# S4 convolution beside a 16-head expert layer on one core: parameters in three parts of channels, gelu for two head groups at once, and tiles from own lists of slots

## The chip, the cores and the metric

The kernel runs on one core of a Trainium2 chip. A core has a matmul engine (TensorE, PE in the profile, with its weight loads listed as PEld), an elementwise engine (VectorE, DVE), an engine for activations (ScalarE, ACT), GpSimd (POOL), which here issues the gathers, and SyncE (SP), which issues most DMA transfers. Each engine works through its own instructions in program order and waits at an instruction until what it needs is there. SBUF is the memory on the chip with 128 partitions; PSUM holds the matmul results in eight banks of 128 x 512 float32.

The metric is device time in microseconds for one execution. Before the change three runs took 755.45, 764.48 and 769.52 us, median 764.48.

## The reference

```python
x  = A_u                                   # 2048 tokens x 448 channels
xn = _layernorm(x)
return x + _A_ref(xn, ...) + _B_ref(xn, ...)

def _A_ref(u, ...):                        # S4 convolution, 256 states per channel
    dt = exp(log_dt); logdA = dt * (A_re + 1j * A_im); dB = dt * (B_re + 1j * B_im)
    K = einsum("dn,dnl,dn->dl", Cc, exp(logdA * l), dB).real     # kernel of length 2048
    y = irfft(rfft(u) * rfft(K))[:2048] + u * Dskip              # causal convolution
def _B_ref(x, ...):                        # 16 heads, one expert of 64 x 64 each
    q = einsum("nd,dhc->nhc", x, w_q)
    s1 = q1 @ k1.T ; s2 = q2 @ k2.T        # 64 scores each, per head
    e = argmax(s1) * 64 + argmax(s2)       # the best of both halves (top 1)
    act = gelu(sum_d(x * u[e]))            # tanh form
    out = sum_h(act * v[e])                # softmax over one candidate is 1
```

## The kernel before, in words

Tokens are cut into 16 tiles of 128. The two halves of the work share all engines and run interleaved.

**The expert half.** The query weights are folded into the keys at the start: for each of 16 heads SP loads w_q in two tiles of 448 KB (L855), PE multiplies them with the keys (wc, L862), ScalarE takes the result out of PSUM (L866), PE transposes it (L875), and ScalarE writes the table W (L881 to L883). Per token tile, PE transposes the normalized tokens (L943) and forms 2048 scores (sc, L961 and L970), VectorE takes maxima (mx, L985) and finds the indices (L992 to L1006). GpSimd then gathers for each token and head one row of u and v side by side, 3584 bytes (ue, L1083). With 32 tokens by 4 heads on the partitions, one token tile needs 16 gathers: 4 groups g of heads by 4 columns c. VectorE forms a dot product per gather (L1091), ScalarE the square and the tanh of gelu (L1098, L1104), VectorE the small steps between (L1101, L1110, L1107, tiles of 128x4) and the product with a mask (A, L1114); PE adds up the v rows (po, L1121), and ScalarE takes them out (ob, L1133). So 64 chains of gelu are formed, one for each tile and group, each behind four gathers.

**The convolution half.** At the start the S4 parameters are worked out for all 448 channels at once, states on the partitions, in tiles of 128x896 (L432 to L499, on VectorE, ScalarE and GpSimd): weights, phases as integers and logarithms of magnitudes. exp(log_dt) is computed from 112x4 values (L364 and on), stored to DRAM and loaded back over all partitions. The phases go to DRAM as tp_d (L502) and the split exponents as tt_d (L508); every four of 56 batches of 8 channels load their share back (tpl, L540; ttl, L520). A batch forms phase rows (ph, L610, L614), sines and cosines on ScalarE (CS, L629 to L635), magnitudes by matmul and Exp (lg L579, mg L590), their products (zi and mg, L660 to L666), and on PE the kernel blocks kp (L682) and VK (L702, L706). The convolution of a chunk of channels then runs on PE with products on VectorE (U L798, us L803, cp L808, ip L830), its output goes through DRAM (t_d, L842; tl, L1149), is multiplied once more (po, L1159) and added to the output by a GpSimd DMA (L1167).

**The order.** The program is a set of streams of steps. A string ORDER, one character per step, fixes the order in which steps are issued, and with it the order on each engine. A step names rings it takes from and gives back to; the rings only count. The tiles themselves come from pools: 25 tiles of 4096 bytes (pool "q") serve the token tiles, W, the gathers, and the tiles of the convolution; PSUM tags kv and s2 have three banks each, tp, po, vk and others one.

```python
t = s.q.tile([128, 1024], F32, name=name, tag="q", bufs=s.NQ)
y = p.add("e_g", "GATHER", xf(128, 3584), ga, deps=[s.ix_done[t]], take=("ue",))
y = p.add("e_p", "PE", 830, m2, deps=[y], take=("po",) if g == 0 else (), give=("A", "ue", "ue", "ue", "ue"))
```

Of the kernel before, what the change touches and what calls it, by code (L numbers as in the profile page):

```python
# [22 lines left out]
NB = 8  # L23
# [92 lines left out]
class Plan:  # L116


    def __init__(s):
        s.streams, s.left, s.phys = {}, {}, {}  # L120

# [26 lines left out]
    def run(s):  # L148
# [3 lines left out]
        for ch in ORDER:  # L152
# [25 lines left out]
    "zUIygU!#ISh!h#yyyISRzKRVROizWx$W$%yyfziHHhNgxSfSzxPxKLISiz!#JM#RjRLRSfI!$$%QzIhhgTJfiIziGISSzMfykI!#yIyU#RUi&hRhh!yI$S$i"
    "dIeRXUSzUO%jhSIUNSlizIIhPkhLRhQzISMLhTMyRdiLzibURe!yyRzMfUzlyUiU##NY!U$$%LShSgJRjyRZZSifMhKhgHzz!UzKxiHfSfaN#Ufyy(LJ!Skh"
    "M#$hOPgUzxUiSL$%RRSyhhyymzxHTMhmlizxUUSRhhhn!nhHjhkhgLMURiUSLhhUyz#gRyRQV1iziSIiNI!fiIzz!ifSYclmISfhM#fQ$I$%hnSSgO#IyTWf"  # L180
    "IiUzjhiKZPhHI!&hRmUIhR#QkW$UhnI$UyyyyUzIzlzU%!hHjRy#z!iziS#Iy$RS$hkJyyyL%ZiUSzzHHdMhyRyLMelIbROzISz!I#!Iy#$SygiPfIhiSSXm"
    "zfzhRJmRUfRU$%L!nITnjhgfi#SIUIfMLhIhMkUIUiSgRRR#h!ISli$$N%OIJjKxcNJhzxyyVhhcyyxSzzSyUySUxzSzh!TPi#h!h#QmULUWZ$aih&Kyyhnf"
    "$UfURfU%MRziSzUgyzyLhNMhRgifSLfRQz!hSiH(yhg#HWzz#h!$R$hhbjZzz%Riyh!k#y!#MHYO$SSd$%iyHPIhekSizIIUSzlliIiRRLjhIKQghTzIUiSh"
    "UIR!#UihISMkhKyIyyfI!UI#URlmyS$I$fURfSShnJVY%NcgROhKxhfSajXxUizzyyPiSxzgLkhyymRQixzz!M#z#N!$Rhym$lhzfinyL&%RTSyzy(njUSUz"
    "hUz!yhhgzhzMU#Uhk!!SWR##il$$fh!Ri%R#hzhJfyi$yzfyxz$OzyfgxSxxS%KfimSiSiUhhP!gL#RMRhjhL#TiUiyUWSd!z$hRUSyzRMR$yy%yhkhSiyhS"
    "izUnjzhkilSROUNY(Qzlh!zhSzUPy&#!y#ymiSR$z$egyUb%hny!h#!aRyzTizfzUgzSfyyRURSXfiUR#$NQSU$UROzUihSSxoz!xYhgmzSf%yzSyP#h#Uy!"
    "h!hyfURRjnhTiRkhhS$U#hyS$y%UiymjUzilk!#UlxV$$xg%&hzzz!zzWh#!(Sn#hRSyyzyiz!iyyRmRS#V#$Wh!my$$inno$fUoyfigSSph%hzfgp%zfzUq"
    "rzqzyyphYj!hhzUrizfiyTkqpqroz#rhhhi#!!dpjqlW#$hrebiUh#kst$!hpg%pqWhxh$iorfoo$qltUxpgypyfzrhqxhciXfUg%irszijhUyifq&pzfrUi"
    "yhkhyyxy(zlzU!thozy#p#!qzz$hy$pjq!hr##iy!z$cay%yhhiyg$yUzfyUhzfqhrzhkpz%qr!pyyygUVzrtWihhuqppl#zfzyghrfi#!hy!ms(#fd#$yqm"
    "hyu!hr$%nqteth$ii$irnyiymjYbxxmhxsihnkxKnhjii%tzhWilgfhhYt&ykzgzzQffzzzz!yhhgh#if#yy!l$fmmh!$#h#!izz%iji$ynhyyuhnhyzkhhl"  # L190
    "z$zzihjgfhzi!hf#z!kayfli#gfifib$ih!hg$mhhuhijd%#hi)heh)(ym!nini#*ki$ljhxzXm%i+hhkf$xzxlxngh%hmgyyyizzifi&f!ynhhjgyy#yyhh"
    "i!khflf#zh$h*$y+hjmnkhca%hzziiilmnYyzg!hiz#y!hhzzyf#$zjgh$chzfykg%yh!zfzfifihdhzl#!hmi#i!eh##nh)o*+jb$i$!i$hg$ihk,%%ix)x"
    "lhhyh*zfmjx+niiyYygykhhyzff,aiyyyzyilgyxy,,yXyzzf!h&zhjmyfklgnz#o#h!zmyhy!n$$p#p!#hhhhqzhq$%zih$izpzizifr%jqprzhpgqrifzf"
# [11 lines left out]
class Kernel:  # L205
# [1025 lines left out]
```

## Time and profile before

| what | value |
|---|---|
| median of three runs | 764.48 us |
| the profiled execution | 763.02 us |
| its span, first to last instruction | 761.1 us |
| mean granted TensorE clock | 0.915 of full |
| busy: PE, DVE, ACT, POOL | 652.1, 669.5, 552.9, 360.7 us |
| ACT table loads at L639 and L590 | 28 and 26, 1283 ns each |
| DMA moved | 211.83 MB, mean 278 GB/s |

The profile lists groups of instructions with busy time, mean duration and the idle time of the engine just before them, with what ended it. Windows give busy time by engine for a stretch of the span, with the granted clock, the mean busy share of the 16 DMA engines, and GB/s. The chain that ended last follows the last instruction back through what released each step.

### The profile page before, as it was taken

The page shows a single profiled execution, that of the slowest core. Times are in us where ns is not written, and L with a number is a line of the kernel's source. Part 1 is how long each engine was busy: PE and PEld are TensorE (multiplying, and loading weights), DVE is VectorE, ACT ScalarE, POOL GpSimd, SP SyncE. Part 2 cuts the span into 40 slices and gives each one's busy share as a digit, 9 for nine tenths or more (in the row PEclk, how much of TensorE's full clock was granted, in tenths as well). Part 3 has the DMA queues.
Part 4 walks back from the last instruction along what each step waited for, and adds up shares of the span by engine and source line. Part 5 has one row for each costly group of instructions (what it writes and reads, how often), then busy time and mean ns, then how long its engine had stood idle before and what let it go on. Part 6 is the DMA issues. An engine that isn't in the chain of part 4 may idle for free.

```text
span 761.1 us, 19861 instructions
## 1 busy us (share of the span) xinstructions
PE 652.1 (86%) x7628; PEld 355.8 (47%) x7628; DVE 669.5 (88%) x1691; ACT 552.9 (73%) x1137; POOL 360.7 (47%) x307
## 2 busy tenths in 40 slices
PE   1999999999999999999887958679996587899882
PEld 0344333443444444444465734346763344576751
DVE  4896578999999999999999999999998999999840
ACT  3886147566876886774796898888898888999630
POOL 2011024544363645655447686484564657752523
PEclk9999999999999999999999877688987756999995
DMA  9998656978687896887989999899898999977998
GB/s 324 328 374 305 228 136 254 355 238 246 221 257 266 252 327 191 309 255 257 337 300 340 281 324 361 263 327 279 265 342 271 308 325 286 339 248 209 296 178 128
DMA packets 119095, 211.83 MB, mean 278 GB/s; under 512 B 38937, under 2 KB 94233, under 8 KB 118937
## 3 DMA queue, kind: packets, MB, share of 16 engines
q0 software_dynamic: 31232, 124.80, 51.6%
q1 hardware_dynamic: 87768, 85.77, 35.2%
q8 instruction: 60, 0.98, 0.5%
q14 instruction: 35, 0.28, 0.1%
HBM read 180.90 MB, written 33.29 MB: 281 GB/s over the span
## 4 chain that ended last, share of the span: by engine, by line
PE 41%; DVE 29%; ACT 14%; DMA 7%; issue 6%; SPq 1%; POOL 1%; POOLq 0%; DVEq 0%; ACTq 0%
PE sc L961 14%; DVE ue L1091 6%; PE U L798 3%; PE po L1121 3%; DVE mg L666 3%; DVE zi L662 3%; DVE ph L614 3%; PE kp L682 3%; PE sc L970 3%; DMA ue<-in_uv_dram,ig 3%; PE ip L830 2%; PE wc L862 2%; PE up L724 2%; ACT CS L629 2%; DMA VU<-vu_d 2%
## 5 line engine op out<-in xcount | busy, mean ns | idle before, releaser
L1083 POOL DMA_INDIRECT ue<-in_uv_dram,ig x256 | 312.6, 1221 | 309.0 <-PE po L1121 72.9
L961 PE MATMUL sc<-W,xt 128*128 128x512 f32 x384 | 180.1, 608 | 2.2 <-ACT xt L946 1.9
L1091 DVE SCALAR_TENSOR_TENSOR ue<-ue,xr 128x448 f32<-128x448 f32 x256 | 154.1, 617 | 4.0 <-DMA ue<-in_uv_dram,ig 4.0
L961 PEld LDWEIGHTS sc<-W,xt 128*128 128x128 f32 x384 | 69.7, 191 | 91.9 <-issue 83.9
L1121 PE MATMUL po<-ue,A 128*32 128x448 f32 x512 | 68.6, 616 | 9.4 <-DVE A L1114 5.0
L590 ACT ACTIVATE mg<-lg 128x512 f32<-128x512 f32 x112 | 63.4, 600 | 11.1 <-PE lg L579 10.6
L682 PE MATMUL kp<-mg 128*32 128x64 f32 x1792 | 62.3, 237 | 7.9 <-DVE kt L693 3.1
L666 DVE TENSOR_TENSOR mg<-mg,CS 128x1024 f32<-128x1024 f32 x56 | 68.2, 1217 | 0.0
L662 DVE TENSOR_TENSOR zi<-mg,CS 128x1024 f32<-128x1024 f32 x56 | 68.2, 1217 | 0.0
L635 ACT ACTIVATE CS<-CS,halfpi 128x1024 f32<-128x1024 f32 x56 | 64.5, 1152 | 0.8
L614 DVE CUSTOM_DVE_ANT_0 ph<-st,ph 128x512 uint16<-128x512 uint16 (+2 forms) x84 | 64.9, 772 | 0.2
L629 ACT ACTIVATE CS<-ph 128x1024 f32<-128x1024 int32 x56 | 62.6, 1118 | 1.4 <-issue 0.5
L632 ACT ACTIVATE CS<-ph 128x1024 f32<-128x1024 int32 x56 | 63.2, 1128 | 0.0
L682 PE MATMUL kp<-zi 128*32 128x64 f32 x1792 | 61.6, 234 | 0.0
L682 PEld LDWEIGHTS kp<-mg 128*32 128x32 f32 x1792 | 45.2, 119 | 29.2 <-issue 11.7
L579 PE MATMUL lg<-lc,rt 32*128 32x512 f32 x112 | 39.8, 548 | 21.5 <-ACT mg L590 17.5
L702 PE MATMUL vp<-f,kt 128*64 128x128 f32 x448 | 43.6, 326 | 16.5 <-ACT tl L1163 5.0
L985 DVE TENSOR_REDUCE mx<-sc 128x8 f32<-128x512 f32 x64 | 43.6, 682 | 14.6 <-PE sc L970 9.2
L682 PEld LDWEIGHTS kp<-zi 128*32 128x32 f32 x1792 | 47.2, 121 | 0.1
L798 PE MATMUL U<-VU,g 128*64 128x128 f32 x384 | 42.3, 301 | 5.4 <-DVE cp L808 2.7
L702 PEld LDWEIGHTS vp<-f,kt 128*64 128x64 f32 x448 | 28.9, 160 | 38.3 <-issue 11.9
L862 PE MATMUL wc<-wq,kk 128*64 128x448 f32 x128 | 31.7, 586 | 17.1 <-DMA wq<-in_wq_dram 17.1
(244 smaller groups left out, 1242.2 us busy)
## 6 DMA issues: line engine op xcount, KB each, us to landing
wq<-in_wq_dram SPq DMA_DIRECT2D x32, 448.0 KB
xr<-xn_d SPq DMA_DIRECT2D x64, 224.0 KB
vu_d<-vst SPq DMA_DIRECT2D x64, 112.0 KB
VU<-vu_d SPq DMA_DIRECT2D x12, 512.0 KB
t_d<-tq SPq DMA_DIRECT2D x24, 256.0 KB
tl<-t_d SPq DMA_DIRECT2D x12, 512.0 KB
ue<-in_uv_dram,ig POOLq DMA_INDIRECT x256, 6.4
xx<-in_x_dram SPq DMA_DIRECT2D x16, 224.0 KB
```

The costliest lines, as they stand in the source:

```text
L614: s.nc.vector.tensor_tensor(out=rw(n, 2 * n), in0=rw(0, n), in1=o["st"][:, k, b0:b0 + 2].rearrange("p b h m x -> p (b h m x)")[:, None].to ...
L629: s.nc.scalar.activation(CS[:, 1].rearrange("p (m r x) -> p m r x", r=16, x=2), four(s.ph), AF.Sin, scale=SC)
L635: s.nc.scalar.activation(B["CS"][:, 0], B["CS"][:, 0], AF.Sin, scale=-SC, bias=s.halfpi)
L662: V.tensor_tensor(out=zi[:, 512:], in0=mg[:, 512:], in1=CS[:, 1], op=ALU.mult)
L666: V.tensor_tensor(out=mg[:, 512:], in0=mg[:, 512:], in1=CS[:, 0], op=ALU.mult)
L682: s.nc.tensor.matmul(kp[32 * c:32 * c + 32, 64 * gi:64 * gi + 64], T[ri][:, 1024 + m:1056 + m], view(T[ri], m, [[512, 2], [1, 32]]), start ...
L702: s.nc.tensor.matmul(vp[64 * ri:64 * ri + 64, 128 * gi:128 * gi + 128], B["kt"][:, 64 * gi:64 * gi + 64], s.f1[:, ri], start=True, stop=True)
L798: s.nc.tensor.matmul(U[64 * h:64 * h + 64, sl, ri], s.g[q][:, 2 * kk + h, ri], src[:, k1 + h, :w], start=True, stop=True)
L961: s.nc.tensor.matmul(B["sc", q].rearrange("p a b -> p (a b)"), B["xt"][:, i], w, start=(q % 2 == 0 and i == 0), stop=(q % 2 == 1 and i == 2))
L1083: s.nc.gpsimd.indirect_dma_start(out=ue, out_offset=None, in_=s.io["uv"], in_offset=bass.IndirectOffsetOnAxis(ap=s.IDX[t][:, c, g:g + 1].b ...
L1091: s.nc.vector.scalar_tensor_tensor(Q["ue", c][:, :D], Q["ue", c][:, :D], 1.0, B["xr", c], op0=ALU.mult, op1=ALU.mult, accum_out=Q["dot"][: ...
L1121: s.nc.tensor.matmul(B["po"][32 * c:32 * c + 32, :D], Q["A"][:, c], Q["ue", c][:, D:], start=(g == 0), stop=(g == 3))
```

## The change

1. **Parameters in parts.** Channels are cut into parts of 128, 160 and 160. Each part has its six inputs packed into one array, loaded as two transfers, and goes through the same arithmetic on tiles of 256, 320 and 320 columns. Part 0 stays on chip: its phases (`R1`) and split exponents (`tt`) are read by the batches where they were formed. Parts 1 and 2 go through tp_d and tt_d as before. exp(log_dt) is computed on 128x448 after one broadcast load, with no way through DRAM.
2. **Gelu for two groups.** From token tile 4 on (`PT=4`) one chain serves two head groups: eight gathers and dots, then small steps on 128x8 and a mask product of 128x256, then two groups of po matmuls. Tiles 0 to 3 keep one chain per group.
3. **Own lists of slots.** The 25 tiles of 4096 bytes and the banks of kv, s2 and tp are allocated once. `run` takes the index that was freed first when a step takes from a ring, and `rel` in a step's code says which tile it frees.
4. A new ORDER string, and 2048 instead of 4096 for the DMA scratch size.

```diff
+PARTS = (128, 160, 160)
...
                 s.left[s.phys[tag]] -= 1
+                if s.phys[tag] in s.free:
+                    s.got.setdefault(tag, []).append(s.free[s.phys[tag]].pop(0))
...
-    "4HH4HH44441444Z4444H606HH414144114H72III2II72II2I2I7728I8I2IJJ22I2I2I2I72KIZ414I82852I24K4I4COP224C4234LMLDHMHHH4LMDCLM4"
+    "013ZHH3HH314Z3353153H33116633HH3H322I2222I2I2II2I2III222I2222I7IJJI3K7IICI7788I2IIL8DC332699I798M7874I77OC8DEC77778I7I9D"
...
+    def slot(s, *tags):
+
+        for tag in tags:
+            if s.p.got.get(tag):
+                r, i = s.p.phys[tag], s.p.got[tag].pop(0)
+                return s.own[r][i]
+    def rel(s, *views):
+
+        for v in views:
+            s.p.freed.append(s.where[v.tensor.name])
...
-            T["ld"] = s.sm.tile([112, 4], F32, name="ld")
-            s.nc.sync.dma_start(T["ld"], io["log_dt"].rearrange("(p f) -> p f", f=4))
+            s.nc.sync.dma_start(T["ld"], io["log_dt"].rearrange("(o f) -> o f", o=1).to_broadcast([128, D]))
...
-        N = 2 * D
-        B = s.pb = {} if part == 0 else s.pb
-        hold = ("cs", "cs", "zi", "zi", "mg", "mg", "c3", "c3", "c3", "vk")
+        d0, w = s.parts[k]
+        N, nb, b0 = 2 * w, w // NB, d0 // NB
+        keep = k == 0
...
+        P["tp_done"] = [c1] if keep else [stp(0, 0, "A_re", [f2]), stp(0, 1, "T3", [ph]), stp(1, 0, "B_im", [f1]), stp(1, 1, "T1", [c1])]
...
-                s.nc.tensor.transpose(o["ps"][:, t], o["tl"][:, t], s.ident)
+                s.nc.tensor.transpose(o["ps"][:, t], P["tt"][t][:, i:i + 4].rearrange("p b k -> p (b k)") if P["keep"] else o["tl"][:, t], s.ident)
...
+            if P["keep"]:
+                o["tp"] = P["R1"][:, :, :, i:i + 4]
...
-        for g in range(4):
+        w = 2 if t >= s.o["PT"] else 1
+        for g0 in range(0, 4, w):
...
+                            for k in ("dot", "x2", "th", "dw"):
+                                Q[k] = s.sm.tile([128, 2, 4], F32, name=k, bufs=2)[:, :w]
...
+            yA = p.chain("e_v2", "DVE", [(75, v2), (dv(128 * w), v2c)], deps=[y, yw, s.C["mask"]], take=("A",), give=("gel",))
+            for g in range(g0, g0 + w):
+                def m2(g=g, g0=g0, Q=Q):
...
+                    s.rel(*[Q["ue", g, c] for c in range(4)])
+                y = p.add("e_p", "PE", 830, m2, deps=[yA], take=("po",) if g == 0 else (), give=(("A",) if g == g0 + w - 1 else ()) + ("ue",) * 4)
```

**What moves, in three places.** The first is SP's list at its start, before. Here pw and pv are parameter tiles, xx token tiles, ld log_dt, kk the keys.

```order
L892 DMA xx<-in_x_dram 128x448 x2
L419 DMA pw<-in_C_im_dram 128x896
L419 DMA pw<-in_B_im_dram 128x896
L419 DMA pv<-in_C_re_dram 128x896
L419 DMA pv<-in_B_re_dram 128x896
L294 DMA ld<-in_log_dt_dram 112x4
L419 DMA pv<-in_A_im_dram 128x896
L419 DMA pv<-in_A_re_dram 128x896
L892 DMA xx<-in_x_dram 128x448 x3
L309 DMA kk<-in_k_dram 128x2x64 x2
L272 DMA ident<-in_ident_dram 128x128
L855 DMA wq<-in_wq_dram 128x896
```

After, a name q with a number is one of the 25 slots; the rows from the lc table to the first two wq loads are shown (ahead of them stand the broadcast of log_dt and four token tiles).

```order
L355 DMA lcf<-in_lc_dram 128x768
L969 DMA q_85<-in_x_dram 128x448
L969 DMA q_86<-in_x_dram 128x448
L342 DMA kk<-in_k_dram 128x2x64
L441 DMA q_87<-in_par_dram 128x1024
L342 DMA kk<-in_k_dram 128x2x64
L359 DMA wtf<-in_wt_dram 128x64
L448 DMA q_88<-in_par_dram 128x2x256
L311 DMA ident<-in_ident_dram 128x128
L929 DMA q_90<-in_wq_dram 128x896
L929 DMA q_91<-in_wq_dram 128x896
```

The six full parameter loads give way to the two of part 0, now behind the token tiles and just ahead of the weights.

The second place is ScalarE in the same stage. Before, the Square, Abs and Sqrt of all channels (L446 to L450) stand in front of the first evictions of PSUM (xt L946, vst L727, wt L866):

```order
L446 ACTIVATE pv<-pw 128x896
L447 ACTIVATE pw<-pw 128x896
L925 ACTIVATE xx<-xx,q,y 128x448 x2
L448 ACTIVATE pv<-pw 128x896
L450 ACT_TABLE_LOAD
L450 ACTIVATE pw<-pv 128x896
L329 ACTIVATE lc<-lcf 128x768
L946 ACTIVATE xt<-xtp 128x512
L727 ACTIVATE vst<-up 128x448
```

After, they are those of part 0 (L486 to L490), and the exponents' first copies (L498) and the arctangent (L516) stand between evictions (L941 for wt, L788 for vst, L1023 for xt):

```order
L486 ACTIVATE q_87<-q_88 128x256
L487 ACTIVATE q_87<-q_88 128x256
L488 ACTIVATE q_87<-q_88 128x256
L941 ACTIVATE wt__250<-kv_104 128x448
L490 ACT_TABLE_LOAD
L490 ACTIVATE q_87<-q_87 128x256
L788 ACTIVATE q_97<-tp_110 128x448
L498 ACTIVATE q_89<-q_88 128x16x8
L364 ACTIVATE wt<-wtf 128x64
L498 ACTIVATE q_89<-q_88 128x16x8
L941 ACTIVATE wt__285<-kv_105 128x448
L516 ACT_TABLE_LOAD
```

Each table load and each wait of part 0 on ScalarE now has evictions behind it that PE's next matmuls need.

The third place is VectorE. Its list around the first product zi of the first batch, before (mx maxima, A the mask product, q and y of the layernorm):

```order
L1091 SCALAR_TENSOR_TENSOR ue,dot<-ue,xr 128x448
L985 TENSOR_REDUCE mx<-sc 128x8
L1107 SCALAR_TENSOR_TENSOR th<-th,dw 128x4
L920 SCALAR_TENSOR_TENSOR y<-q,y 128x2
L1114 TENSOR_TENSOR A<-mask,th 128x128
L918 TENSOR_TENSOR q<-y 128x2
L992 TENSOR_TENSOR eq<-sc,mx 128x512
L660 SCALAR_TENSOR_TENSOR zi<-mg,CS 128x512
```

and after (s with a number is a score bank):

```order
L669 TENSOR_SCALAR ph<-q_88 128x2x2x16 x2
L501 TENSOR_TENSOR q_99<-q_98,q_99 128x20x8
L1065 TENSOR_REDUCE mx<-s_108 128x8
L1111 SCALAR_TENSOR_TENSOR ix<-cm,tf 128x8x4
L1072 TENSOR_TENSOR q_83<-s_108,mx 128x512
L673 ISA ph<-ph,st 128x256
L1120 TENSOR_TENSOR top<-top 128x32
L719 SCALAR_TENSOR_TENSOR zi<-mg,CS 128x512
```

The phase rows read part 0's tile (q_88) instead of a reloaded one, steps of another part (L501) stand among them, and 17 score maxima stand ahead of this zi, where 15 did.

In the second half, the gelu steps of VectorE before:

```order
L1110 TENSOR_TENSOR dw<-dot,ig 128x4
L1091 SCALAR_TENSOR_TENSOR ue,dot<-ue,xr 128x448
L614 ISA ph<-ph,st 128x256
L1091 SCALAR_TENSOR_TENSOR ue,dot<-ue,xr 128x448
L660 SCALAR_TENSOR_TENSOR zi<-mg,CS 128x512
L1107 SCALAR_TENSOR_TENSOR th<-th,dw 128x4
L614 ISA ph<-st,ph 128x512
L1114 TENSOR_TENSOR A<-mask,th 128x128
L693 TENSOR_TENSOR kt<-kp,dsk 128x2
L1101 SCALAR_TENSOR_TENSOR x_7339<-x_7339,dot 128x4
L1110 TENSOR_TENSOR dw<-dot,ig 128x4
```

and after:

```order
L1186 SCALAR_TENSOR_TENSOR x_5960<-x_5960,dot 128x8
L1176 SCALAR_TENSOR_TENSOR q_97,dot<-q_97,xr 128x448
L1195 TENSOR_TENSOR dw<-dot,ig 128x8
L673 ISA ph<-st,ph 128x1024
L1176 SCALAR_TENSOR_TENSOR q_98,dot<-q_98,xr 128x448
L1192 SCALAR_TENSOR_TENSOR th<-th,dw 128x8
L1176 SCALAR_TENSOR_TENSOR q_85,dot<-q_85,xr 128x448
L1199 TENSOR_TENSOR A<-mask,th 128x256
```

Two chains of four small rows each have become one, and more dots stand between its steps.

More of the change, by code (lines that the diff above doesn't have):

```diff
@@ L165, in run @@
             st.fn()
+            if sorted(r for r, _ in s.freed) != sorted(s.phys[tag] for tag in st.give if s.phys[tag] in s.free):
+                raise RuntimeError("slots: " + k)
+            for r, i in s.freed:
+                s.free[r].append(i)
+            s.freed = []
         if any(pos[k] < len(s.streams[k]) for k in names):
@@ L178 @@
[L178 to L181, printed above, removed]
@@ L235, in alloc @@
         s.vkp = pool("vkp")
-        s.q = pool("q", s.NQ)
+        s.q = pool("q")
         s.ps = pool("ps", 1, space=bass.MemoryType.PSUM)
+        s.own = dict(ue=[s.q.tile([128, 1024], F32, name="q%d" % i) for i in range(s.NQ)])
+        for tag, n in s.bufs.items():
+            s.own[tag] = [s.ps.tile([128, 512], F32, name="%s%d" % (tag, i)) for i in range(n)]
+        s.where = {}
+        for r, l in s.own.items():
+            s.p.free[r] = list(range(len(l)))
+            for i, t in enumerate(l):
+                s.where[t[:, :8].tensor.name] = (r, i)
         dr = pool("dr", 1, space=bass.MemoryType.DRAM)
@@ L425, in params @@
+        held = 3 if keep else 4
+        l1 = p.add("par_ld", "SP", xf(128, 4 * N * per), ld1, take=("ue",))
+        l2 = p.add("par_ld", "SP", xf(128, 4 * N * (6 - per)), ld2, take=("ue",) * (held - 1))
         d1, d2 = dv(N), dv(N, 2)
@@ L516, in exponents @@
         o = {}
+        i = 4 * g - P["b0"]
         def l():
@@ L607, in f @@
                 b0 = b % 4
+                if k == 3 and b % 4 == 2 and "ue" in o["give"]:
+                    s.rel(o["tp"])
                 if k < 0:
```

357 lines of the change are left out of this document (204 added, 153 removed).

## The prediction

> **What bounds the kernel now.** I began with the page's first two parts: totals, then the span in forty slices.
>
> ```profile
> span 761.1 us, 19861 instructions
> PE 652.1 (86%) x7628; PEld 355.8 (47%) x7628; DVE 669.5 (88%) x1691; ACT 552.9 (73%) x1137; POOL 360.7 (47%) x307
> PE   1999999999999999999887958679996587899882
> DVE  4896578999999999999999999999998999999840
> PEclk9999999999999999999999877688987756999995
> ```
>
> No engine is full on average, but the slices are not alike: TensorE (PE) is full up to about slice 19, VectorE (DVE) from slice 7 to slice 37. Averages over stages hide this, so next come 20-us windows; the five pairs are PE, PEld, DVE, ACT, POOL with busy time and instruction count, then clock, DMA share, GB/s.
>
> ```profile
> 60.00:80.00 20.00, 20.00 (x81) 8.69 (x82) 10.70 (x16) 8.56 (x26) 2.23 (x1) 1.00 0.90 328
> 80.00:100.00 20.00, 18.79 (x55) 7.70 (x54) 10.39 (x16) 5.68 (x21) 0.00 (x0) 1.00 0.41 136
> 100.00:120.00 20.00, 19.31 (x56) 7.67 (x55) 16.32 (x39) 8.32 (x24) 9.17 (x9) 1.00 0.77 251
> 120.00:140.00 20.00, 20.00 (x67) 7.39 (x66) 17.56 (x62) 15.82 (x36) 10.53 (x9) 1.00 0.67 224
> 300.00:320.00 20.00, 20.00 (x146) 8.18 (x143) 19.97 (x53) 14.57 (x30) 12.88 (x12) 1.00 0.88 272
> 440.00:460.00 20.00, 11.63 (x183) 7.29 (x186) 18.60 (x53) 18.09 (x35) 15.68 (x14) 0.69 0.99 346
> 500.00:520.00 20.00, 14.58 (x254) 9.26 (x246) 17.21 (x49) 16.44 (x30) 16.66 (x14) 0.83 1.10 307
> 560.00:580.00 20.00, 12.31 (x178) 7.32 (x182) 15.78 (x45) 18.84 (x34) 6.93 (x7) 0.68 0.89 325
> ```
>
> Three stages follow. Up to 140 us PE is full and DVE is not: these four windows leave DVE 80 − 54.97 = 25.0 us idle. From 140 to about 360 both are full. From 360 to 720 PE falls to 12 to 15 us in 20 in the quoted windows while DVE stays near 20; there DVE sets the pace, and in the dips neither does. The last slice (19 us) holds no DVE work: a chain of transfers. The chain that ended last agrees (by engine, by line, some of its pieces):
>
> ```profile
> PE 41%; DVE 29%; ACT 14%; DMA 7%; issue 6%; SPq 1%; POOL 1%; POOLq 0%; DVEq 0%; ACTq 0%
> by line: PE sc L961 13.6%; DVE ue L1091 6.3%; issue 5.9%; PE U L798 3.2%; PE po L1121 3.1%; DVE mg L666 3.0%; DVE zi L662 2.9%; DVE ph L614 2.8%; PE kp L682 2.7%; PE sc L970 2.6%; DMA ue<-in_uv_dram,ig 2.6%; PE ip L830 2.5%; PE wc L862 2.4%
> 3.56 6.87 DMA ld<-in_log_dt_dram
> 447.58 8.55 DMA ue<-in_uv_dram,ig
> 512.87 6.16 DMA ue<-in_uv_dram,ig
> 550.22 4.82 DMA ue<-in_uv_dram,ig
> 736.01 4.91 DMA t_d<-tq
> 741.06 2.89 DMA tl<-t_d
> ```
>
> PE's largest item is the score matmuls, DVE's are dots and products, and 2.6% (20 us) is gathers whose landing was awaited, 19.5 us of it in the three pieces shown, two of them in windows where DVE dips.
>
> **The change, part by part.** All sums stand against this execution: 763.02 us, its span of 761.1 and 1.9 us around it. It lies 1.5 us below the median of 764.48; the shown runs spread by 14 us, so 2% (15 us) is about what a measurement can tell from no change.
>
> *Gelu for two groups.* The first view is groups by line (busy, mean ns, idle before), the second a stretch of DVE's timeline, start and duration.
>
> ```profile
> L1101 DVE SCALAR_TENSOR_TENSOR x<-x,dot 128x4 f32<-128x4 f32 x64 | 9.9, 154 | 6.3 <-ACT x L1098 6.0
> L1110 DVE TENSOR_TENSOR dw<-dot,ig 128x4 f32<-128x4 f32 x64 | 10.0, 157 | 0.0
> L1107 DVE SCALAR_TENSOR_TENSOR th<-th,dw 128x4 f32<-128x4 f32 x64 | 9.9, 154 | 5.0 <-ACT th L1104 4.1
> L1114 DVE TENSOR_TENSOR A<-mask,th 128x128 f32<-128x128 f32 x64 | 18.3, 287 | 2.7 <-PE po L1121 2.0
> L1091 DVE SCALAR_TENSOR_TENSOR ue<-ue,xr 128x448 f32<-128x448 f32 x256 | 154.1, 617 | 4.0 <-DMA ue<-in_uv_dram,ig 4.0
> L1104 ACT ACTIVATE th<-x 128x4 f32<-128x4 f32 x64 | 13.3, 208 | 13.8 <-DVE x L1101 13.7
> ```
> ```profile
> 132.24 0.15 DVE L1101 SCALAR_TENSOR_TENSOR x<-x,dot 128x4 f32<-128x4 f32 x1
> 132.31 0.16 DVE L1110 TENSOR_TENSOR dw<-dot,ig 128x4 f32<-128x4 f32 x1
> 132.38 0.28 DVE L1003 TENSOR_TENSOR eq<-eq 128x256 bf16<-128x256 bf16 x1
> ```
>
> From token tile 4 on, 48 chains become 24. Three small DVE instructions go per merged pair. A listed duration is 0.155 us, but the next instruction starts 0.07 us later, so one is worth 0.07 on a full engine: 24 × 3 × 0.07 = 5.0 us (11.2 by listed durations). The mask product A: from 128 to 448 columns the rows go from 287 to 617 ns, about 1.03 ns a column, so 128x256 is near 0.42 us, against 2 × 0.287: 0.155 listed per pair, or 0.07 by starts; 24 × 0.07 = 1.7 us (3.7 listed). Together 6.7 us, up to 14.9. I take 6.7, since DVE is full there. "Perfetto Trace Analysis" of the Trainium skill, section "Optimizing Scalar/DVE Operations", says a DVE instruction on SBUF carries about 60 ns of overhead and that profiled latency is about twice this since half overlaps the next instruction. The trace agrees (0.07 from start to start, 0.155 listed); by its 60 ns the saving would be an estimated 24 × 4 × 0.06 = 5.8 us, by the full latency the larger sum.
>
> Each chain also waits twice for ScalarE, 11.3 us over 64; 24 fewer give 4.2 if the wait per chain stays. Together 10.9 us. Between 220 and 360 us, where roughly a quarter of these chains lies (judged from the tiles' spread), PE is full and hides the gain; so 8 us reach the end, with 0 as the other end if the order refills the gaps. On ScalarE 48 activations go: 48 × 0.208 = 10 us, in cover.
>
> *Gather slots.* A pair holds eight slots of 4096 bytes, where a single held four, until its po matmuls; part 0 holds two of 25 until its last steps are formed. The waits and the DMA issues:
>
> ```profile
> POOL ue L1083 <- PE po L1121: 72.9, 23, 9.5
> ue<-in_uv_dram,ig POOLq DMA_INDIRECT x256, 6.4
> ```
>
> GpSimd waits for a slot today, 9.5 us at worst, and DVE hardly notices: 4.0 us before 256 dots. So slots are tight with cover. Doubling the 20 us of awaited landings is the upper end; the lower is that the 4.0 us vanish, because the own list hands out the slot that was freed longest ago. I take +2, near the small row. PSUM lists I cost at nothing: number and length of the PE instructions stay, and a bank's release is still its last reader; they share the gather term's ends.
>
> *Parameters in parts.* About 31 DVE instructions of 128x896 become three each, of 256, 320 and 320 columns; the 19 for log_dt go from 112x4 to 128x448; 10 table loads come on ScalarE.
>
> ```profile
> L438 DVE SCALAR_TENSOR_TENSOR pv<-pw,pv 128x896 f32<-128x896 f32 x2 | 2.2, 1092 | 0.1
> L435 DVE TENSOR_SCALAR pv<-pv 128x896 f32<-128x896 f32 x2 | 1.2, 623 | 0.0
> L639 ACT ACT_TABLE_LOAD x28 | 35.9, 1283 | 0.4
> L639 ACT ACTIVATE dum<-one 128x1 f32<-128x1 f32 x28 | 5.7, 203 | 0.3
> ```
>
> The columns stay; each split adds two fixed parts. 617 ns at 448 and 1092 at 896 columns leave 0.14 listed, 0.08 by starts: 31 × 2 × 0.08 = 5.0 us (8.7 listed). log_dt: nine at 0.617 and ten at half of 0.623 make 8.7 us, against 19 × 0.155 = 2.9: +5.8. So 10.8 to 14.5 us more DVE work, nearly all ahead of 140 us, under the 25.0 us of idleness; I cost it at 0, and at 10.8 if that cover fails, since from 140 on DVE is full. Ten loads are 12.8 us of ScalarE, whose quoted windows from 60 to 140 are 38.4 of 80 busy. "ScalarE: Activation LUTs" of the Trainium skill, section "What ACT_TABLE_LOAD costs", puts a switch at 1283 ns plus a drain of about 1380: 26.6 us for ten. The load agrees at 1283; a separate drain does not show, since the instruction behind 28 loads waited 0.3 us in all. By the page ScalarE would carry 13.8 us more, an estimate that ScalarE's 41.6 idle us in those windows would still cover.
>
> Keeping part 0 on chip removes four of the 14 reloads of each kind (tpl, ttl) and the wait for log_dt's way through DRAM. Is the first product earlier for it? These are DVE around it, then the first weight transfer and its matmul:
>
> ```profile
> 124.02 0.68 DVE L985 TENSOR_REDUCE mx<-sc 128x8 f32<-128x512 f32 x1
> 125.69 0.68 DVE L660 SCALAR_TENSOR_TENSOR zi<-mg,CS 128x512 f32<-128x512 f32 x1
> 11.44 0.34 SPq L855 DMA_DIRECT2D wq<-in_wq_dram  x1
> 16.42 0.98 PE L862 MATMUL wc<-wq,kk 128*64 128x448 f32 x1 [16.42 <-DMA wq<-in_wq_dram]
> ```
>
> In program order the first zi stands behind 15 score maxima before, behind 17 now. Maxima come at PE's pace, PE is full, and the score matmuls ahead of them are the same. So the product does not come earlier, though DVE has more done by then.
>
> *Head.* Ahead of the first wq transfer SP now issues about 1.06 MB less (six parameter loads of 448 KB become 512 + 256 KB; one x tile, the 384-KB lc and the 224-KB broadcast come ahead); the 60–80 us window moves 328 GB/s, or 328 KB a microsecond, so 3.2 us. Against it, ScalarE's queue has part 0's Square, Abs and Sqrt ahead of the PSUM evictions that PE needs; they wait for parameters issued just before wq, and a late landing of 6.87 us (the log_dt row) would hold PE by as much. I take −1, between −3.2 and +6.9, since the two pull against each other. Being PE's start, this shifts all behind it.
>
> *Tail.* The t_d store, tl load and output adds stay in the same sequence: 0.
>
> Sum: 763.0 − 8 + 2 − 1 = **756 us**.
>
> **Rivals.**
> *Slower: slots run out.* Where pairs of gathers fill the pool while the convolution also takes tiles (about 360 to 700 us), the first dot of a pair finds its row not landed. For it speaks GpSimd's 72.9 us of waiting for po; against it, only 4.0 us reach DVE. It decides once DVE's queued work between a po and the dot that reuses its slot falls below the issue-to-landing time of 6.4 us. Twice today's 20 us on the chain, with the gelu gain intact: 756 + 20 − 2 = 774; with that gain eaten by eight-dot groups that start late: 782.
> *ScalarE blocks the head.* Part chains and table loads sit ahead of evictions; PE starves near 20 to 60 us: 756 + 1 + 6.9 = 764, with the DVE cover also gone 775.
> *Faster: the dips fill.* The windows 440, 500 and 560 leave 1.40 + 2.79 + 4.22 = 8.4 us of DVE idle. If own lists and the new order issue gathers early enough, these go, with the full 3.2 us of head: 756 − 8.4 − 2.2 = 745.
> *Nothing comes of it.* The maxima still pace the first product, gelu's gaps are refilled: 763.
>
> **How the numbers follow.** Forecast near 756: 0.32; nothing: 0.15; ScalarE's head: 0.10; faster: 0.20; slots: 0.23. Under 749 (2%) lie the faster case and a quarter of the forecast's spread, in which the listed durations come true: 0.28. Over 780 lie two thirds of the slot case and a third of the head's, where both miss together: 0.19. The rest, 0.53, is within 2%. The range's low end is the faster case with the 8.2 us between the two readings of the gelu rows, 745 − 8.2 = 737; the high end is the slot case at 782 with the head's −1 lost and the 1.5 us to the median: 784.
>
> **What would show it.** Right: 40 chains, small 128x8 rows near 0.16 us, A near 0.42; the first zi still near 125 us; DVE at 19 or more of 20 from 140 to about 710; `ue` waits on DVE under 8 us; the tail as now. Wrong: DVE idle before dots of 15 us or more in several windows past 360; the first wc later than 16.4 or PE idle between 20 and 60; the first zi clearly before 120 us; or a granted clock so different that PE paces the second half.

## The result and the profile after

The changed kernel took 790.74 us in the median of six runs (788.36 to 796.26), the kernel before 765.88 in six. The ratio is 1.043, with a 95% interval of 1.036 to 1.050: slower by 25 to 33 us, and outside the forecast range. The profiled run of the changed kernel has a span of 793.6 us. The page's totals and two of its rows of slices:

```profile
span 793.6 us, 19725 instructions
PE 648.0 (82%) x7628; PEld 357.1 (45%) x7628; DVE 671.8 (85%) x1667; ACT 565.7 (71%) x1121; POOL 379.4 (48%) x315
PE   2999996699999999999987868589965838998850
DVE  5704989999999999989999999999989978998500
```

Busy time of PE and DVE is what it was (652.1 and 669.5 before). The 32 us are idle time. Two places stand out against the rows before: DVE's third slice is 0 where it was 9, and PE's seventh and eighth are 6 where they were 9. The windows show it in microseconds, first one of the kernel before, then of the changed one (PE, PEld, DVE, ACT, POOL):

```profile
40.00:60.00 20.00, 19.82 (x96) 8.47 (x96) 17.77 (x28) 18.24 (x45) 2.91 (x2) 1.00 1.02 379
```
```profile
40.00:60.00 20.00, 19.99 (x93) 8.27 (x92) 1.78 (x4) 13.48 (x42) 0.00 (x0) 1.00 0.96 320
80.00:100.00 20.00, 19.08 (x52) 7.90 (x53) 19.86 (x40) 11.22 (x30) 2.91 (x1) 1.00 0.02 7
120.00:140.00 20.00, 12.79 (x42) 4.59 (x41) 19.86 (x45) 15.88 (x33) 7.72 (x8) 0.91 0.56 171
140.00:160.00 20.00, 14.02 (x42) 5.48 (x42) 19.80 (x61) 14.61 (x24) 9.38 (x8) 0.74 0.58 203
```

DVE did 17.8 us of work between 40 and 60 us before and 1.8 now; what it did not do there it does from 80 us on, where it is now full. PE loses 13 us in the two windows from 120 to 160. Its timeline names the waits, and DVE's names the first products:

```profile
130.23 1.64 PE L1211 MATMUL po<-q,A 128*32 128x448 f32 x8 [3.56 <-DVE A L1199]
145.73 1.72 PE L1211 MATMUL po<-q,A 128*32 128x448 f32 x8 [8.43 <-DVE A L1199]
```
```profile
152.73 0.68 DVE L719 SCALAR_TENSOR_TENSOR zi<-mg,CS 128x512 f32<-128x512 f32 x1
159.52 1.22 DVE L725 TENSOR_TENSOR mg<-mg,CS 128x1024 f32<-128x1024 f32 x1
```

The first zi comes at 152.7 instead of 125.7 us. The first mg product, the last of its batch, is the milestone used below: 159.5 now, and before

```profile
144.59 1.21 DVE L666 TENSOR_TENSOR mg<-mg,CS 128x1024 f32<-128x1024 f32 x1
```

So 15 us are lost by then. The last batch's mg product is 20 us late (733 against 712), and the end 32 us. The other large piece is therefore the tail. GpSimd's timeline there, before and after; x1 is one DMA that adds a block of the convolution to the output (the row with ob adds a token tile of the expert half), the bracket is what GpSimd waited for:

```profile
749.16 1.27 POOL L1167 DMA_DIRECT2D out_dram<-tl  x1 [0.70 <-ACT tl L1163]
754.16 1.27 POOL L1167 DMA_DIRECT2D out_dram<-tl  x1 [3.73 <-ACT tl L1163]
756.01 1.29 POOL L1167 DMA_DIRECT2D out_dram<-tl  x1 [0.57 <-ACT tl L1163]
```
```profile
763.14 1.28 POOL L1253 DMA_DIRECT2D out_dram<-q  x1 [4.46 <-issue]
769.10 1.28 POOL L1253 DMA_DIRECT2D out_dram<-q  x1 [4.69 <-issue]
774.56 0.88 POOL L1221 DMA_DIRECT2D out_dram<-ob  x1 [4.18 <-issue]
...
780.44 1.29 POOL L1253 DMA_DIRECT2D out_dram<-q  x1 [3.69 <-issue]
784.39 1.27 POOL L1253 DMA_DIRECT2D out_dram<-q  x1 [2.66 <-issue]
788.45 1.29 POOL L1253 DMA_DIRECT2D out_dram<-q  x1 [2.79 <-issue]
```

Before, each add waits for ScalarE's copy of its block. Now most wait for "issue", nothing that the profile shows, and follow each other at 4 to 6 us. SP's last tl load, which feeds them, is near in both:

```profile
746.82 0.49 SPq L1149 DMA_DIRECT2D tl<-t_d  x1
```
```profile
766.44 0.43 SPq L1234 DMA_DIRECT2D q<-t_d  x1
```

From there to the span's end it is 14.3 us before and 27.2 after: 13 us in the tail.

The waits of the changed kernel that bear on the forecast's other terms (total us, times, longest):

```profile
POOL q L1168 <- PE po L1211: 111.4, 27, 11.7
DVE mx L1065 <- PE s L1050: 18.9, 4, 16.4
DVE q L1176 <- DMA q<-in_uv_dram,ig: 13.3, 7, 5.6
DVE q L1072 <- PE kv L936: 13.2, 1, 13.2
```

DVE waits 13.3 us for gathered rows instead of 4.0. The second and fourth rows hold two waits of 16.4 and 13.2 us: DVE stands at the first score maximum from 36 to 52 us and at its comparison until 67, with parameter parts 1 and 2 behind them in its queue. Part 1 could not have filled the gap either: in SP's list its loads stand behind the last weight loads and go out at 60.5 us.

```profile
54.93 4.83 SPq L929 DMA_DIRECT2D q<-in_wq_dram  x6
60.53 0.58 SPq L441 DMA_DIRECT2D q<-in_par_dram  x1
```

### The profile page after: what moved, and what is told of

It reads as the page before. It is cut to its first block, busy times and chain, and to the rows that moved or that the text cites. A ratio compares the mean times of both kernels' runs of the same rounds, so it can differ in the third digit from the quotient of the medians.

```text
span 793.6 us, 19725 instructions
## 1 busy us (share of the span) xinstructions
PE 648.0 (82%) x7628; PEld 357.1 (45%) x7628; DVE 671.8 (85%) x1667; ACT 565.7 (71%) x1121; POOL 379.4 (48%) x315
## 5 line engine op out<-in xcount | busy, mean ns | idle before, releaser
L1168 POOL DMA_INDIRECT q<-in_uv_dram,ig x256 | 327.1, 1278 | 258.4 <-PE po L1211 111.4
L1039 PE MATMUL s<-q,xt 128*128 128x512 f32 x384 | 181.2, 612 | 2.8 <-ACT xt L1023 2.7
L1176 DVE SCALAR_TENSOR_TENSOR q<-q,xr 128x448 f32<-128x448 f32 x256 | 153.2, 619 | 13.4 <-DMA q<-in_uv_dram,ig 13.3
L1039 PEld LDWEIGHTS s<-q,xt 128*128 128x128 f32 x384 | 70.4, 193 | 94.8 <-issue 87.7
L1211 PE MATMUL po<-q,A 128*32 128x448 f32 x512 | 70.0, 631 | 23.8 <-DVE A L1199 15.7
L741 PE MATMUL kv<-mg 128*32 128x64 f32 x1792 | 63.7, 239 | 17.2 <-DVE mg L725 9.9
L646 ACT ACTIVATE mg<-kv 128x512 f32<-128x512 f32 x112 | 62.7, 598 | 14.2 <-PE kv L635 12.4
L688 ACT ACTIVATE CS<-ph 128x1024 f32<-128x1024 int32 x56 | 62.6, 1118 | 11.9 <-DVE ph L673 11.8
L741 PE MATMUL kv<-zi 128*32 128x64 f32 x1792 | 63.1, 237 | 2.2 <-issue 2.2
L741 PEld LDWEIGHTS kv<-mg 128*32 128x32 f32 x1792 | 46.8, 121 | 38.5 <-issue 14.4
L741 PEld LDWEIGHTS kv<-zi 128*32 128x32 f32 x1792 | 48.2, 122 | 2.4 <-issue 2.3
L1253 POOL DMA_DIRECT2D out_dram<-q x16 | 22.1, 1383 | 50.1 <-issue 18.7
```

The costliest lines, as they stand in the source:

```text
L646: s.nc.scalar.activation(mg[:, :2, i], ps.rearrange("p (k n) -> p k n", k=2), AF.Exp)
L741: s.nc.tensor.matmul(kp[32 * c:32 * c + 32, 64 * gi:64 * gi + 64], T[ri][:, 1024 + m:1056 + m], view(T[ri], m, [[512, 2], [1, 32]]), start ...
L1039: s.nc.tensor.matmul(B["sc", q].rearrange("p a b -> p (a b)"), B["xt"][:, i], w, start=(q % 2 == 0 and i == 0), stop=(q % 2 == 1 and i == 2))
L1168: s.nc.gpsimd.indirect_dma_start(out=ue, out_offset=None, in_=s.io["uv"], in_offset=bass.IndirectOffsetOnAxis(ap=s.IDX[t][:, c, g:g + 1].b ...
L1176: s.nc.vector.scalar_tensor_tensor(Q["ue", g, c][:, :D], Q["ue", g, c][:, :D], 1.0, B["xr", c], op0=ALU.mult, op1=ALU.mult, accum_out=Q["d ...
L1211: s.nc.tensor.matmul(B["po"][32 * c:32 * c + 32, :D], Q["A"][:, g - g0, c], Q["ue", g, c][:, D:], start=(g == 0), stop=(g == 3))
```

## The experiments

Runs e1 to e12 were made on chips on which the kernel before itself takes 830 to 841 us, e13 to e18 on chips where it takes 764 to 765. Only ratios to the kernel before on the same chip are compared, and times within one chip. The first theory: (a) parameter work that stood in the wq phase now meets the first gelu chains and holds PE, 15 us; (b) the halved DMA scratch spaces the output adds, 13 us.

### Taking the two suspects away: e13, e14, e15, e17

e13 is the changed kernel itself. e14 leaves part 2's steps out:

```diff
+        for n, (a, b) in dict(par_ld=(4, 6), par_g=(8, 12), par_v=(50, 75), par_a=(22, 33), par_v2=(22, 33), par_st=(6, 12), par_f=(2, 3)).items():
+            for st in s.p.streams[n][a:b]:
+                st.fn, st.take, st.give = (lambda: None), [], []
```

e15 adds, and e17 has alone, the old scratch size, with room made by

```diff
-        s.dt = c.tile([128, D], F32, name="dt")
+        s.dt = s.vkp.tile([128, 4096], F32, name="dt", tag="vk", bufs=1)[:, :D]
...
-    nc = bacc.Bacc("TRN2", target_bir_lowering=False, num_devices=1, dynamic_dma_scratch_size=2048)
+    nc = bacc.Bacc("TRN2", target_bir_lowering=False, num_devices=1, dynamic_dma_scratch_size=4096)
```

> The changed kernel, as the yardstick on the same chip: ratio to the kernel before 1.03 to 1.045, first mg product at 160 us.

> The changed kernel with all steps of part 2 left out (loads, slots, arithmetic, stores); the batches of part 2 read part 1's phases and exponents, so their work keeps its size and only its values are wrong. Theory: part 2 as a whole is the 16 us; the first mg product comes at 143 to 147 us and the time falls by 13 to 20 us against the control. Rival: part 2 is only half of it (the order of PE and the pairs' slots the rest): 150 to 155 us, and 5 to 10 us.

> Part 2 left out as in the run beside it, and the DMA scratch at 4096. If part 2 and the scratch are the whole difference, the ratio to the kernel before is 0.99 to 1.01; if the gelu pairs or the own slots cost more besides, it stays above 1.015.

> The changed kernel with the DMA scratch back at 4096 once more. From the run without part 2 (17.8 us between the two sizes) 772 to 778 us where the kernel before takes 764 (ratio 1.012 to 1.02); if the scratch gave that much only because part 2 was gone, 780 or more.

| kernel | median us | before beside it | ratio (95%) |
|---|---|---|---|
| e13, changed | 791.69 | 764.34 | 1.037 (1.029 to 1.046) |
| e14, without part 2 | 778.32 | 764.34 | 1.016 (1.008 to 1.023) |
| e15, without part 2, scratch 4096 | 760.55 | 764.34 | 0.994 (0.990 to 0.998) |
| e17, scratch 4096 | 772.79 | 764.93 | 1.011 (1.007 to 1.015) |

Part 2 is worth 13.4 us (791.69 − 778.32), the scratch 17.8 us without part 2 and, on the other chip, 1.037 − 1.011 = 2.6%, some 20 us, with it. The two add: 31.1 us for both together, against 27.4 us between the changed kernel and the one before. Without both the kernel is 3.8 us faster than the one before; but e15 does less work than either, since part 2 is missing from it, so this is no gain of a complete kernel. e15 and e17 also move the tile of exp(log_dt); e2 below has the size alone.

In e14 DVE's milestone is back where it was before, and PE's two waits for A are nearly gone:

```profile
145.23 1.23 DVE L725 TENSOR_TENSOR mg<-mg,CS 128x1024 f32<-128x1024 f32 x1
```
```profile
127.04 0.96 PE L1211 MATMUL po<-q,A 128*32 128x448 f32 x8 [0.43 <-DVE A L1199]
134.04 1.14 PE L1211 MATMUL po<-q,A 128*32 128x448 f32 x8 [1.78 <-DVE A L1199]
```

In e17 the output adds wait for ScalarE again, as before the change; the row "out_dram L1253 <- issue", 18.7 us in the changed kernel, is gone from the waits:

```profile
POOL out_dram L1252 <- ACT q L1247: 18.2, 7, 5.8
POOL out_dram L1252 <- ACT th L1188: 14.8, 1, 14.8
POOL out_dram L1220 <- issue: 4.1, 1, 4.1
```

From the last tl load to the span's end it is 29.0 us in e13 and 28.9 in e14, and 12.4 in e17 and 11.7 in e15. So in these profiled executions the tail is 16.6 and 17.1 us shorter with 4096, nearly all of the scratch's 18 to 20 us.

### The scratch from the other side: e1, e2

e1 is e17 on a chip of the first group; e2 is the kernel before with 2048.

```diff
-    nc = bacc.Bacc("TRN2", target_bir_lowering=False, num_devices=1, dynamic_dma_scratch_size=4096)
+    nc = bacc.Bacc("TRN2", target_bir_lowering=False, num_devices=1, dynamic_dma_scratch_size=2048)
```

> The changed kernel with the DMA scratch back at 4096 (to make room, the tile of exp(log_dt) lies in the space that VK uses later). Theory: the halved scratch makes GpSimd's queue take the last output adds 4 to 6 us apart, where none of them had anything else to wait for; the last add then comes within about 8 us of the last tl load, as before, and the time falls by 10 to 13 us, to 778 to 781. Rival: the adds are apart because the tail's transfers share the DMA engines; then nothing changes, 788 to 794.

> The kernel before with only the DMA scratch halved to 2048. Theory of the scratch: its last eight output adds move 4 to 6 us apart and the time rises by 8 to 13 us, to 774 to 779. Rival (scratch is nothing): 764 to 768.

e1 came to 852.38 us beside 830.12; its times spread from 838 to 864, which gives no ratio. In its trace it is 11.8 us from the last tl load to the end, as in e17. e2 came to 855.30, a ratio of 1.032 (1.025 to 1.038), 25 us by the medians, more than the 8 to 13 expected. The kernel before now shows the changed kernel's mark, which it did not have:

```profile
POOL out_dram L1167 <- issue: 19.5, 5, 6.6
```

From the last tl load to the end e2 takes 24.5 us instead of 14.3. That is 10 of its 25 us; where the other 15 lie stays open, since there is no trace of the kernel before from such a chip to set beside it.

"DMA: Bandwidth & Descriptors" of the Trainium skill, section "SWDGE vs HWDGE vs iDMA", says that GpSimd writes its DMA descriptors into rings that lie in a part of SBUF. That agrees with a size that is taken from SBUF here; that half of it costs some 18 us, only these runs show, and why the adds move apart none of them shows.

### What part 2 does there: e6, e9, e10

e6 leaves out 42 of 76 VectorE instructions of parts 1 and 2, e9 replaces their table functions, e10 does both.

```diff
-                                     (6.35 * N, lambda: V.reciprocal(B["B_im"], B["B_im"])),
+                                     (6.35 * N, lambda: None if k else V.reciprocal(B["B_im"], B["B_im"])),
...
-        at = p.add("par_a", "ACT", ac(N), lambda: A.activation(B["B_im"], B["B_re"], AF.Arctan), deps=[m], tset="A")
+        at = p.add("par_a", "ACT", ac(N), lambda: A.activation(B["B_im"], B["B_re"], AF.Arctan if keep else AF.Copy), deps=[m], tset="A")
```

> The changed kernel with 42 of VectorE's 76 instructions of 320 columns for parts 1 and 2 left out (those that overwrite their own input, the four reciprocals among them): about 27 us of listed VectorE time less, nearly all between 68 and 155 us. ScalarE, its table loads, GpSimd, the loads and the order stay, and the convolution's values are not computed rightly. Theory (VectorE's work was moved behind its idle stretch, and PE waits for it at 130 and 146 us): the first mg product comes 10 to 16 us earlier and the time falls by 10 to 20 us against the changed kernel beside it. Rival (ScalarE's table loads and PE's order cause those stalls): under 4 us.

> The changed kernel with ScalarE's Sqrt, Arctan, Ln and Exp for parts 1 and 2 replaced by Square and Copy of the same size, which need no table: 62 table loads instead of 72, the work on VectorE and the order unchanged; the convolution's values are not computed rightly. Theory that the seven loads between 128 and 147 us hold the gelu steps that PE's po waits for: the first mg product comes 4 to 9 us before 160 us. Rival (VectorE's part 2 holds them): under 2 us.

> Both: the 42 VectorE instructions of parts 1 and 2 left out and their tables replaced. If VectorE and ScalarE hold each other up there (each alone was covered by the other), the first mg product comes 12 us or more before 160 us and the time falls by 10 to 16 us against the changed kernel, a ratio to the kernel before near 1.015 to 1.025; if PE's order alone is the cause, 155 us as with VectorE's part alone.

The first mg product came at 155.2, 159.0 and 152.6 us: 4.3, 0.5 and 6.9 us gained, where 10 to 16, 4 to 9 and 12 or more were expected. On the time nothing shows: e6 took 859.71 beside the changed kernel's 860.47 on that chip, e10's ratio of 1.043 has an interval of 1.025 to 1.061, and e9 (885.16 beside 840.88) has no ratio. The theory that VectorE's work alone is the 15 us fell. The traces show why. In e6 DVE, relieved, waits at the same place for ScalarE, which still has part 2's chain and its tables:

```profile
134.62 0.49 DVE L532 TENSOR_TENSOR q<-q 128x320 int32<-128x320 f32 x1 [3.28 <-ACT q L522]
...
138.95 0.16 DVE L1192 SCALAR_TENSOR_TENSOR x<-x,dot 128x4 f32<-128x4 f32 x1 [2.67 <-ACT x L1189]
```

In e10, with both relieved, it waits for the gathered rows of the second group, which GpSimd issued late:

```profile
131.03 0.63 DVE L1182 SCALAR_TENSOR_TENSOR q<-q,xr 128x448 f32<-128x448 f32 x1 [1.01 <-DMA q<-in_uv_dram,ig]
...
134.15 0.62 DVE L1182 SCALAR_TENSOR_TENSOR q<-q,xr 128x448 f32<-128x448 f32 x1 [1.23 <-DMA q<-in_uv_dram,ig]
```

Part 2 still held its four slots there; that the gathers waited for those is argued, not shown. PE's longest wait for A is still 6.8 us in e10, against 8.4. VectorE's steps, ScalarE's chain and, as far as that argument goes, the gathers stand in series under one po matmul, each covering the next. At this place in the order only the removal of all of part 2 (e14) gives the 15 us.

### Moving the parts: e3, e11, e16

Only the order string differs: the same letters, those of part 1 or of part 2 at other places (e11 and e16 also have scratch 4096). e3 takes part 1 into DVE's idle stretch; e11 puts part 2 300 places later, e16 later and spread over twice as many places.

```diff
-    "K77S997S8SE7FES7EMF877887FGR9R9xZ88RO9II9689II7SPS78RbRS79R7T7R797U779I7SU9SRRSHQ8HOcI7U87SSxZZS7I7SPUTReRR7IU7aUUUUUUIS"
...
```

> The changed kernel with the order string alone changed: part 1's loads go ahead of the last wq loads, and its arithmetic ahead of the first score maximum, where VectorE stood idle from 36 to 67 us. Theory: the 16 us were lost because VectorE had nothing to do there and did part 1 later, where it is full; the first mg product comes 8 to 15 us earlier than 160 us, and the time falls by as much, to 776 to 783. Rival: PE's stalls at 130 and 146 us come from where po stands in PE's order, or from ScalarE behind table loads; then the first mg product moves by under 4 us and the time stays at 787 to 794.

> The changed kernel with scratch 4096 and part 2's steps (loads, arithmetic, stores) 300 places later in the order string, behind the first products; nothing is left out. If the loss is that part 2 meets the first gelu chains and PE's po, the first mg product comes 10 us or more earlier than 160 us; the time then falls by 5 to 12 us beyond what the scratch gives, if VectorE has room for part 2's 16 us later, and by 0 to 4 if it is full there too.

> The changed kernel with scratch 4096 and part 2's steps later and spread over twice as many places of the order string, behind the first products; nothing left out. If part 2 costs its VectorE time wherever it stands, the first mg product comes at 145 to 147 us and the time is that of the changed kernel with scratch 4096 (ratio 1.015 to 1.03); if there is room later, 1.00 to 1.01.

e3 is a miss: 888.36 us, a ratio of 1.062 (1.049 to 1.076), and the first mg product comes at 187.2 us, later instead of earlier. Part 1's loads and slots now stand before the weights: SP has issued the last weight load at 89 us instead of 60, and PE waits for weights in many places:

```profile
PE kv L936 <- DMA q<-in_wq_dram: 26.5, 10, 13.7
```

So it tells nothing on VectorE; it shows that part 1 at this earlier place holds back wq. In e11 and e16 the first mg product is at 145.3 and 146.4 us, as in e14, but with nothing left out: the 15 us hang on where part 2 stands. But the loss returns with interest. Batch 4's mg product is at 249 and 238 us against 224 and 225 in e1 and e13, and the ratios are 1.065 (1.030 to 1.099) and 1.069 (1.061 to 1.077). e16 is 44 us slower than e17 by ratio. Its windows from 180 to 280 us have PE at 13 to 14 of 20:

```profile
180.00:200.00 20.00, 13.85 (x43) 5.80 (x43) 10.59 (x34) 7.88 (x16) 5.50 (x6) 0.85 0.66 205
...
260.00:280.00 20.00, 12.57 (x94) 5.25 (x94) 13.23 (x43) 8.23 (x14) 5.60 (x6) 0.73 0.53 150
```

Over these 100 us PE is busy 67.7 us and DVE 70.7, in e17 98.0 and 96.2: neither engine paces the stage. These orders were shifted by rule, not planned, so they do not show that no good later place exists; they show that part 2 at these two places between running products costs more than the 13 us that it costs now.

### Gelu in pairs: e4, e5, e7, e12, e18, e8

e4 does each merged instruction as two halves in the same places; e5 is the changed kernel beside e6 to e8. e7, e12 and e18 are one kernel, the one before with pairs (and scratch 3584 for room). e8 is the changed kernel with singles.

```diff
+                for g in range(w):
+                    s.nc.vector.scalar_tensor_tensor(Q["th"][:, g], Q["th"][:, g], 1.0, Q["dw"][:, g], op0=ALU.add, op1=ALU.mult)
...
-    OPT = dict(UE=11, XX=4, CS=2, ZI=2, MG=4, KT=4, HL=2, SG=1, XR=4, OB=3, XT=1, ST=1, PT=4)
+    OPT = dict(UE=11, XX=4, CS=2, ZI=2, MG=4, KT=4, HL=2, SG=1, XR=4, OB=3, XT=1, ST=1, PT=16)
```

> The changed kernel with each merged gelu instruction (128x8, mask product 128x256) done as two of half the width, in the same places; gathers, dots and the order stay. It undoes the merging alone: 96 more small VectorE instructions, 48 more on ScalarE. If VectorE paces the second half, start to start 6.7 us are lost (4 to 8: 795 to 799); if the listed durations count, 11 to 15 us (802 to 806); if VectorE waits there anyhow, nothing (0 to 3).

> The changed kernel itself once more, as the yardstick for the runs beside it on the same chip. Ratio to the kernel before near 1.043.

> The kernel before with gelu for two head groups from tile 4 on and nothing else changed but what this needs: the order string with the first group's small steps moved to the second's place, and a DMA scratch of 3584 instead of 4096 for room. If pairing pays as forecast (6.7 to 11 us of VectorE, 2 lost to gather slots), the ratio to before is 0.985 to 0.995; if the eight held slots cost more than the instructions save, it is 1.00 to 1.02, and VectorE waits for gathers over 10 us instead of 4.

> The kernel before with gelu in pairs once more, as the candidate to be faster than both: ratio to the kernel before 0.99 to 1.00; under 0.995 with an interval below 1 would make it the fastest version.

> The kernel before with gelu in pairs, as the candidate to be faster than both: ratio to the kernel before 0.99 to 1.00; with an interval below 1 it is the fastest complete version.

> The changed kernel with one gelu chain for each head group again in all tiles; the first group's steps and its po matmuls are put as many steps behind its dots as the pair's are behind its own, the rest of the order stays. If pairing pays, this is 6 to 12 us slower than the changed kernel beside it; if pairing costs by holding slots, it is 3 to 10 us faster, and GpSimd's wait for po falls from 111 us toward 73.

e4: 869.14 us, ratio 1.048 (1.042 to 1.053), beside no run of the changed kernel on that chip; e5 on another chip of the group: 860.47, ratio 1.033 (1.021 to 1.045). The difference of 8.7 us would fit the forecast's 6.7, but the intervals overlap: not settled. Pairs in the kernel before gave 0.996 (0.990 to 1.002), 1.016 (0.999 to 1.033) and, on the faster chip, 1.027 (1.022 to 1.033), 21 us slower. There DVE waits four times as long for gathered rows as before the change (15.4 us against 4.0):

```profile
DVE ue L1092 <- DMA ue<-in_uv_dram,ig: 15.4, 11, 2.7
```

That is 11 us more of waiting, at most 11 of the 21 us; the rest was not taken apart, and this order too was made by rule. The loss lies between the first mg product and the last, 591.3 us apart in e18 and 567.8 before; the scratch of 3584 has no part in it that the tail would show (11.6 us from the last tl load to the end). Why the same kernel lost nothing in e7 is not known. e8 took 900.25 us, 40 more than e5. It is no clean reversal, since its small steps follow each other more closely: DVE waits 42.8 us for gelu's square instead of 14.0 in e5.

```profile
DVE x L1187 <- ACT x L1184: 42.8, 23, 6.2
```

No complete version was faster than the kernel before; e15, which is, leaves part 2 out.

## Why the prediction was wrong

**The parameter step was the first to fail.** "Nearly all ahead of 140 us, under the 25.0 us of idleness; I cost it at 0, and at 10.8 if that cover fails". The cover failed, at 13.4 us (e14). The 25 us were read from the trace before, as if they would still be there. But they lay beside a DVE that had already done 17.8 us between 40 and 60; in the new order DVE waits there, 16.4 and 13.2 us, and since part 1's loads go out only at 60.5 us, behind the weights, its work is due in the windows that I counted as free. The order showed it: part 1's and part 2's steps stand behind the first maxima in DVE's list. The mechanism is also wider than DVE: ScalarE's chain, and perhaps the gathers, stand in series behind the same po (e6, e9, e10). That the place of part 2 makes the loss is shown for the first product (e11, e16); no run gets the 13.4 us back with part 2's work kept.

**The scratch was not costed at all.** It stood in the list of the change as its last line, and "Tail: the same sequence: 0" looked at the order of steps alone. It is the larger half: 17.8 us (e14 against e15), of which the tail shows 17.1.

**Gelu.** Durations came as worked out: 128x8 instructions 0.159 to 0.165 us, the mask product 0.421 against "near 0.42".

```profile
L1199 DVE TENSOR_TENSOR A<-mask,th 128x256 f32<-128x256 f32 x24 | 10.1, 421 | 0.2
L1186 DVE SCALAR_TENSOR_TENSOR x<-x,dot 128x8 f32<-128x8 f32 x24 | 3.9, 164 | 7.4 <-ACT x L1183 7.4
L1192 DVE SCALAR_TENSOR_TENSOR th<-th,dw 128x8 f32<-128x8 f32 x24 | 3.8, 159 | 0.4 <-ACT th L1189 0.2
```

DVE's waits for ScalarE in gelu are 10.2 us over 40 chains (7.4 and 0.4 here, 0.6 and 1.8 for the singles) where 11.3 over 64 were. At first sight the 4.2 us for fewer waits did not come. But 7.2 of the 10.2 us are one wait of the last chain, behind DVE's last products of the convolution:

```profile
760.58 0.17 DVE L1186 SCALAR_TENSOR_TENSOR x<-x,dot 128x8 f32<-128x8 f32 x1 [7.17 <-ACT x L1183]
```

The other 39 chains wait 3.0 us together, so up to that chain the waits fell by more than forecast; what the last wait costs is not shown.

**Slots.** +2 was mis-sized: DVE waits 9.3 us more for gathered rows (13.3 against 4.0), within the stated ends. It varies: 10.7 us in e13, 6.3 in e15. Gelu and slots together bring nothing that can be seen: from the first mg product to the last it is 567.8 us before, 573.1 after, 568.4 in e13 and 568.5 in e15 (one execution each), where −8 and +2 were forecast. DVE in the stage from 360 to 720 us is busy 342.95 us, as much as before (343.18): no gap was closed. That the longer waits for rows eat gelu's saving is argued from these sums; no run separates the two. The forecast also read DVE as staying near 20 us in the windows quoted past 360; the rows say 18.60, 17.21 and 15.78, so DVE was not the pace in all of them.

**Right** were the head (the first weight matmul is at 13.9 instead of 16.4 us, the thirteenth maximum 1.6 us earlier) and the lengths of the merged instructions. That the first product would not come earlier is right by luck: it was to stay near 125 us behind maxima at PE's pace, and it came at 152.7, because steps of part 2 stand in DVE's list between the sixteenth maximum (129.3) and the seventeenth (151.1). The signs "`ue` waits on DVE under 8 us" (13.3) and "the tail as now" (27.2 us from the last tl load instead of 14.3) failed too. Of the rivals, none was the one: slots running out pays 9 of the 27 us at most; ScalarE's head names in its last words, "with the DVE cover also gone", the step that failed, but ties it to PE starving from 20 to 60 us, where PE is busy 38.7 of 40 us; and neither names the tail. PE idles from 120 to 160.

## What to carry to other kernels

Idle time in the trace before is cover only for work that stays ahead of the same in-order waits; before counting it, read where the new order puts the work behind a wait of that engine, and what memory the work needs to start. Every line of a diff gets a term, buffer sizes of queues first, since they change no instruction and so show in no list. Where several engines stand in series under one instruction, relieving one shows the next, and only removing the whole tells the price.

## What was not expected of the hardware

Halving the DMA scratch from 4096 to 2048 makes GpSimd's last output adds follow at 4 to 7 us, with 18.7 to 19.6 us of waits that name no releaser, in both kernels (e2 and e13; one gap in e2 is 9 us). The same two programs take 8 to 9% longer on some chips than on others (764 against 830 us before, 791 against 860 after). On the slower ones the first mg product comes at the same time, 160 us (e5 and e13). What is late there is the later stage: PE shows 36.0 us of waits before the kp matmuls that name no releaser (e5), against 1.9 us in two waits on the others (e13). The kernel before shows the same there, 28.2 us in 68 waits (e2, with 2048). The cause was not found.

```profile
PE kv L741 <- issue: 36.0, 84, 1.1
```
